# RWKV-7 attention followed by a hard-swish feed-forward: 64-row turns from unit 4 on, and one PSUM pair in place of two single banks

## The chip, the cores and the metric

The program runs on one core of one Trainium2 chip. A core has TensorE (PE in the profile: matmuls and transposes, and PEld, its weight loads), VectorE (DVE), ScalarE (ACT), GpSimd (POOL) and SyncE (SP, which only issues DMAs here). PE writes to PSUM, 8 banks of 512 float32 columns on 128 partitions; DVE and ACT read from there. The metric is the device time of one execution in microseconds (us).

## The reference

Everything is float32. Four batches, 8 heads, 768 tokens, head size 40. First a recurrence over tokens, per batch and head, with a 40x40 state:

```python
for t in range(S):
    y[:, :, t] = np.einsum('bhd,bhde->bhe', rt, state)
    Sa = np.einsum('bhde,bhe->bhd', state, at)
    state_decay = state * wt[:, :, None, :] - np.einsum('bhd,bhe->bhde', Sa, bt)
    state = state_decay + np.einsum('bhd,bhe->bhde', vt, kt)
```

Its output, laid out as 3072 tokens by 320 features, goes through a feed-forward layer with 2048 hidden features:

```python
h = x @ w_in
relu6 = np.clip(h + 3.0, 0.0, 6.0)
g = h * relu6 / 6.0
return g @ w_out
```

## The kernel before, in words

**Units.** The recurrence is done in chunks of 64 tokens. A *unit* is one chunk of two batches: 128 rows (64 tokens of each batch on 64 partitions) with 8 heads of 40 features. There are 24 units, 0 to 23 (`NK`), in groups of four (`NU`). The triangular systems of a group (64 by 64 for each head and batch) are inverted together on DVE, in some 60 small products and sums (`invert`, `prod` and `x` in the profile); the 64-blocks are completed from 32-blocks by two small PE steps (`third_block`, here z and t, each copied out of PSUM by four ACT copies, `zs` and `tinv`).

**The stages of a unit.** `prepare` makes a unit's own factors ahead of time: W turns the decay w (features onto partitions), copies it to the scan's input and DVE scans it (`prods`, L571); `gam` makes the running products; A, B and K turn a, b and k, and DVE multiplies each by a running product (`at` L615, `bt` L623, `kt` L703); F, E, EV and `factor` are further products. `step` does the recurrence: RT and VT turn r and v (ACT copies them out), S turns the state, R is at times the state (DVE adds EV, L888), C the masked scores of v and r (DVE masks them, L546), U and UT apply the inverse, rS is r times the state, H masked scores again, and `ysn` (L1021) yields the output and the new state; DVE adds both (L1028, L1032). move/move2 send the output by DMA to `xt`, the input of the feed-forward.

**Two kinds of turn.** `turn_pairs` makes four PE transposes of 128 rows by 128 columns (L486) into one PSUM bank. `turn_halves` makes eight of 64 rows by 128 columns (L496), on the upper and lower half of PE's rows by turns, into two banks, a pair. Before, a, b, r and v are turned by halves (a and b from unit 8, r and v from unit 4); w, k and the state always as 128 rows.

**Feed-forward jobs.** A job is (unit, half of the hidden features). `expand` makes 48 products (L1124) into two h banks, among them 16 of 64 rows (`short`); ACT and DVE make `gt` from each bank (L1139, L1140). `contract` (L1165) multiplies gt by w_out, 8 products of 320 columns. The contraction of a job is issued after the expansion of the next one. Before, the two jobs of a unit add up in the same bank `o`, and ACT copies the sum out once (`ob`, L1183), then two DMAs store it.

**The order.** It is written out by hand: each engine runs its instructions in the order in which the program issues them, and waits for semaphores on the way. From unit 4 on, four *blocks* j = 0 to 3 pass per unit. In each block `together` is called twice (the unit's own stages and those ahead); it issues the PE work of all its stages in the order of PRODUCTS, then the reads by ACT and DVE in the order of RESULTS. Between these calls `feed` issues pieces of the feed-forward at a rate given per block, with steps of the inversion beside them. In block 0 stand RT, VT, W and the ysn of the unit before; in block 1 S, A, B, R and C; in block 2 U, UT, rS, F; in block 3 H.

**PSUM.** From unit 2 on: bank `one` (128-row turns), bank `o` (feed-forward sums), two pairs `pair` (everything of the recurrence, `ps_pair`), two banks `h`. A tile of PSUM is given out again when the reads of its former owner are done, and its first PE write waits for that.

## Time and profile before

| | us |
|---|---|
| median of three runs (lowest, highest) | 787.39 (785.52, 788.26) |
| the profiled execution | 785.4 |
| its span, first to last instruction | 783.7 |
| PE busy | 725.0 |
| DVE busy | 486.6 |
| ACT busy | 320.2 |
| POOL busy | 171.9 |

By stretch of the span, PE's busy time and granted clock:

| stretch, us | PE busy | DVE busy | clock |
|---|---|---|---|
| 0 to 120 | 75.5 | 102.2 | 0.79 |
| 120 to 200 | 76.2 | 64.3 | 0.98 |
| 200 to 300 | 95.6 | 64.9 | 1.00 |
| 300 to 645 | 342.9 | 225.3 | 1.00 |
| 645 to 784 | 134.8 | 30.0 | 1.00 |

Unit 4 begins at about 190 us. In the profile a group's row gives busy time, the mean duration of one instruction, and the idle time of its engine ahead of it. A matmul's end is modelled and overlaps the next one's start, so what a group of matmuls costs PE is read from start to start in the timeline, not from its duration.

### The profile page before, as it was taken

How to read it: one execution, taken by the hardware profiler on the slowest of the kernel's cores; microseconds unless marked ns; L12 is line 12 of the kernel's file. 1: busy time of each engine (PE TensorE's matmuls, PEld its weight loads, DVE VectorE, ACT ScalarE, POOL GpSimd, SP SyncE). 2: the span in 40 equal slices, each digit the busy share in tenths (PEclk: the TensorE clock that was granted, in tenths of full speed). 3: DMA queues.
4: the chain of work that ended last, by engine and by line, in shares of the span. 5: the costliest groups of instructions: out<-in, count | busy, mean ns of one | idle time of the engine just before them, and what ended most of it. 6: DMA issues, size and time to landing. Idle time of an engine off the chain costs nothing.

```text
span 783.7 us, 32780 instructions
## 1 busy us (share of the span) xinstructions
PE 725.0 (93%) x14552; PEld 613.3 (78%) x14552; DVE 486.6 (62%) x951; ACT 320.2 (41%) x664; POOL 171.9 (22%) x321
## 2 busy tenths in 40 slices
PE   5636788999999989999999999999999999999998
PEld 3625677878878778888788888888888888888886
DVE  7899967688546699345888336887436972223110
ACT  2386865324445334443334543334543234412211
POOL 6403111222232304121304212203212111110000
PEclk9855899999999999999999999999999999999999
DMA  9684554311333312223213223213221101110000
GB/s 123 116 202 123 113 168 69 68 27 35 58 59 63 67 33 48 50 49 66 41 38 58 46 51 64 44 30 60 49 55 39 26 5 30 30 29 10 12 20 18
DMA packets 174205, 44.87 MB, mean 57 GB/s; under 512 B 157424, under 2 KB 172784, under 8 KB 174064
## 3 DMA queue, kind: packets, MB, share of 16 engines
q1 hardware_dynamic: 169760, 42.03, 27.5%
q8 instruction: 115, 1.88, 1.0%
q10 hardware_dynamic: 4304, 0.74, 0.6%
q14 instruction: 26, 0.21, 0.1%
HBM read 34.08 MB, written 3.93 MB: 49 GB/s over the span
## 4 chain that ended last, share of the span: by engine, by line
PE 77%; DVE 10%; issue 6%; DMA 2%; ACT 2%; POOL 2%; SPq 1%; POOLq 0%; ACTq 0%; DVEq 0%
PE h L1124 27%; PE o L1165 25%; PE pair L1021 4%; PE pair L524 4%; PE pair L496 2%; PE one L486 2%; DVE prods L571 2%; PE pair L884 2%; PE pair L925 1%; PE pair L717 1%; DVE prod L769 1%; PE pair L964 1%; DVE x L775 1%; PE pair L980 1%; PE one L906 1%
## 5 line engine op out<-in xcount | busy, mean ns | idle before, releaser
L1124 PE MATMUL h<-xt,win 128*128 128x128 f32 (+1 forms) x2304 | 248.7, 281 | 4.5 <-DVE gt L1140 4.5
L1124 PEld LDWEIGHTS h<-xt,win 128*128 128x128 f32 (+1 forms) x2304 | 229.3, 191 | 22.6 <-issue 4.2
L1165 PE MATMUL o<-wout,gt 128*128 128x320 f32 x768 | 230.5, 443 | 0.0
L1165 PEld LDWEIGHTS o<-wout,gt 128*128 128x128 f32 x768 | 138.4, 190 | 50.9 <-issue 0.2
L1140 DVE SCALAR_TENSOR_TENSOR gt<-gt,h 128x512 f32<-128x512 f32 x96 | 62.0, 680 | 73.4 <-ACT gt L1139 73.4
L1139 ACT ACTIVATE gt<-h,three 128x512 f32<-128x512 f32 x96 | 62.9, 687 | 102.8 <-PE h L1124 102.3
L546 DVE COPY_PREDICATED area<-mask,pair 128x512 f32<-128x512 int32 x56 | 40.4, 724 | 62.2 <-PE pair L524 52.8
L769 DVE TENSOR_TENSOR prod<-x 128x30 f32<-128x30 f32 (+9 forms) x180 | 65.5, 364 | 8.9 <-POOL x L754 3.3
L775 DVE TENSOR_TENSOR x<-x,prod 128x30 f32<-128x30 f32 (+9 forms) x180 | 64.3, 357 | 5.5
L1029 POOL TENSOR_TENSOR yg<-ys,gam 128x512 f32<-128x512 f32 x20 | 25.4, 1272 | 126.1 <-DVE ys L1028 83.2
L690 POOL TENSOR_TENSOR KBt<-K,rgt 128x320 f32<-128x320 f32 x22 | 19.1, 870 | 151.4 <-ACT rgt L679 139.9
L571 DVE TENSOR_TENSOR_SCAN prods<-area,start 128x528 f32<-128x528 f32 x24 | 40.8, 1703 | 9.7 <-ACT area L567 9.6
L1028 DVE TENSOR_TENSOR ys<-pair,ys 128x512 f32<-128x512 f32 x20 | 13.8, 690 | 49.8 <-PE pair L1021 40.8
L862 ACT ACTIVATE RT<-pair 128x512 f32<-128x512 f32 x22 | 13.1, 597 | 54.5 <-PE pair L496 54.4
L722 ACT ACTIVATE EV<-pair 64x320 f32<-64x320 f32 x44 | 18.9, 430 | 36.9 <-PE pair L717 36.5
L1021 PE MATMUL pair<-area,KBt 64*64 64x104 f32 x1280 | 33.1, 252 | 0.0
L1183 ACT ACTIVATE ob<-o 128x320 f32<-128x320 f32 x22 | 9.6, 437 | 56.2 <-PE o L1165 37.8
L837 ACT ACTIVATE tinv<-pair 32x256 f32<-32x256 f32 x48 | 18.0, 375 | 34.7 <-PE pair L827 34.2
L582 DVE TENSOR_TENSOR_SCAN area<-area,start 128x528 f32<-128x528 f32 x24 | 31.1, 1297 | 0.8
L1021 PEld LDWEIGHTS pair<-area,KBt 64*64 64x64 f32 x1280 | 29.1, 133 | 1.4
L950 POOL COPY area<-V 128x320 f32<-128x320 f32 x20 | 9.1, 455 | 84.6 <-DVE area L612 52.9
L600 POOL COPY rgam<-prods 128x256 f32<-128x256 f32 x22 | 24.9, 1131 | 0.0
(286 smaller groups left out, 1049.9 us busy)
## 6 DMA issues: line engine op xcount, KB each, us to landing
V<-in_v_dram SPq DMA_DIRECT2D x96, 40.0 KB
out_dram<-ob SPq DMA_DIRECT2D x47, 80.0 KB
R<-in_r_dram SPq DMA_DIRECT2D x92, 40.0 KB
B<-in_b_dram SPq DMA_DIRECT2D x42, 80.0 KB
K<-in_k_dram SPq DMA_DIRECT2D x42, 80.0 KB
W<-in_w_dram SPq DMA_DIRECT2D x37, 80.0 KB
A<-in_a_dram SPq DMA_DIRECT2D x37, 80.0 KB
xt<-yg SPq DMA_DIRECT2D x72, 40.0 KB
```

The lines of the kernel that those rows point to most:

```text
L524: nc.tensor.matmul(out=o[i][half(q), n ^ (2 * q * placed), :], lhsT=lhs[half(i, D), n ^ (2 * q * swap), half(q)], rhs=rhs[half(i, D), n, h ...
L546: nc.vector.copy_predicated(out=x[:].rearrange("p (i h) t -> p i h t", i=2), mask=mask8, data=o[2])
L571: nc.vector.tensor_tensor_scan(out=prods[:].rearrange("p r m i -> p (r m i)"), data0=wm[:, 0:SCAN], data1=start[:], initial=0.0, op0=ALU.m ...
L582: nc.vector.tensor_tensor_scan(out=back, data0=back, data1=start[:], initial=0.0, op0=ALU.mult, op1=ALU.add)
L769: nc.vector.tensor_tensor(out=pv, in0=_ap(x[:], (i + 1) * L + i, [[L, n], [0, i]]), in1=_ap(x[:], i * L, [[0, n], [1, i]]), op=ALU.mult,)
L775: nc.vector.tensor_tensor(out=rest, in0=rest, in1=pv, op=ALU.add)
L1021: nc.tensor.matmul(out=both[q][half(s), pr, :], lhsT=o[name][half(q), h * D:h * D + SLOT], rhs=beside[name][half(q), 4 * rs + 2 * (s ^ (q ...
L1029: nc.gpsimd.tensor_tensor(out=yg[:], in0=m["ys"][:].rearrange("p r q t -> p r (q t)"), in1=o["G"][:], op=ALU.mult)
L1124: nc.tensor.matmul(out=hp[c][:, i, :], lhsT=lhsT, rhs=rhs, start=(begun[c] == 0), stop=(begun[c] == 3 * NQ - 1))
L1139: nc.scalar.activation(out=gt[:], in_=hp[c][:], func=AF.Relu, bias=three[:], scale=1.0)
L1140: nc.vector.scalar_tensor_tensor(out=gt[:], in0=gt[:], scalar=6.0, in1=hp[c][:], op0=ALU.min, op1=ALU.mult)
L1165: nc.tensor.matmul(out=op[:], lhsT=gts[c][:, n, :], rhs=wout[:, c * HJ + r * NQ + n, :], start=((split or r == 0) and c == 0 and n == 0), ...
```

## The change

It concerns units 4 to 23. The state (unit 4 on), w and k (unit 8 on) are turned as 64-row halves into a pair. `factor` turns 40 in place of 64 rows of each half. The banks `one` and `o` are given back before unit 4, and a third pair, `third`, takes their place. It is the first pair that a `together` call of a unit's own stages takes in blocks 0 and 1 (so W and RT, or S and A, lie in it), and `contract` takes it for its sum. Since no sum can stay there, each job's sum leaves PSUM: the first job's is copied by ACT to an SBUF tile `part`, the second is added to it by DVE, which makes `ob`. `settle` issues the rest of a begun contraction before blocks 0 and 1; the pieces so issued are taken off the following `feed`. In block 1 the turn of k moves up behind that of b. The deferred 64-row products (`short`) come ahead of the turns, no longer behind them.

```diff
+    single = tc.tile_pool(name="single", bufs=1, space=PSUM, side="right")
+    alone = single.__enter__()
     def bank(tag, shape, bufs):
-        return ps.tile(shape, F32, name=tag, tag=tag, bufs=bufs)
+        return alone.tile(shape, F32, name=tag, tag=tag, bufs=bufs)
...
+    def begun_third():
+        single.__exit__(None, None, None)
+        pools["third"] = ctx.enter_context(tc.tile_pool(name="third", bufs=1, space=PSUM, side="right"))
...
         def w_stage():
-            wt = turn_pairs(o["WN"])
+            wt = turn_halves(o["WN"])[2] if halves else turn_pairs(o["WN"])
...
+            if halves:
+                for n in range(2):
+                    x = wt[:, :, :, n * HB:(n + 1) * HB]
+                    nc.scalar.activation(
+                        out=wv[:, :, n, 1:HB + 1].rearrange("p (r q) i -> p q r i", q=2),
+                        in_=x if n else x[:, :, :, ::-1], func=AF.Copy)
+                scan(wm)
+                return
...
         def factor_stage():
             if halves:
-                rg = ps_pair(NPR, SLOT)
+                rg = ps_pair(NPR, D)
...
         def k_stage():
-            x = turn_pairs(o["KN"])
+            x = turn_in(o["KN"], halves)
             yield PE
             kt = o["kt"] = turned("kt")
-            nc.vector.tensor_tensor(out=kt[:], in0=x[:], in1=o["rg"][:], op=ALU.mult)
+            for y, z, g in zip(parts_of(kt, halves), x, parts_of(o["rg"], halves)):
+                nc.vector.tensor_tensor(out=y, in0=z[:], in1=g, op=ALU.mult)
...
         def s_S():
+            if i >= NU:
+                sp = ps_pair(NPR, D)
+                for n in range(NPR):
+                    for x in range(2):
+                        nc.tensor.transpose(
+                            out=sp[x][:, n, :], identity=ident[half(x, D), half(x, D)],
+                            in_=st[half(x, D), n // 2, 2 * (n % 2):2 * (n % 2) + 2, :].rearrange("p r d -> p (r d)"))
+                yield PE
+                S = m["S"] = beside["S"]
+                nc.scalar.activation(out=S[:].rearrange("p q j (x d) -> p x (q j) d", x=2)[:, :, :, 0:D], in_=sp[2],
+                                     func=AF.Copy)
+                return
...
     def contract(i, r, gts):
-        split = i < SPLIT
-        if r == 0 or split:
+        spill = "third" in pools
+        split = i < SPLIT or spill
+        if spill:
+            op = pools["third"].tile([P, 2, 512], F32, name="third", tag="third", bufs=1)[:, 0, 0:DM]
+        elif r == 0 or split:
             op = bank("o", [P, 512], 1)[:, 0:DM]
         else:
             op = sums.pop(i)
+        held[0] = "contract"
...
             if split:
-                part = ffn.tile([P, 3 * P], F32, name="part", tag="xt", bufs=6)[:, 0:DM]
+                part = beside["part"] if spill else \
+                    ffn.tile([P, 3 * P], F32, name="part", tag="xt", bufs=6)[:, 0:DM]
                 nc.scalar.activation(out=part, in_=op[:], func=AF.Copy, scale=1.0 / 6.0)
...
+    def settle():
+        while held[0]:
+            owed[0] -= 1
+            next(stream)
...
-    AHEAD_STAGES = [["W", "gam"], ["A", "B"], ["F", "K"], ["E", "factor"], [], [], [],
+    AHEAD_STAGES = [["W", "gam"], ["A", "B", "K"], ["F"], ["E", "factor"], [], [], [],
                     ["EV"]]
...
-    PRODUCTS = ["W", "S", "K", "RT", "VT", "A", "B", "factor",
-                "ysn", "EV", "R", "C", "U", "UT", "rS", "H", "E", "F"]
-    RESULTS = ["RT", "ysn", "W", "VT", "EV", "R", "S", "C", "A", "B", "move", "move2",
-               "U", "UT", "rS", "F", "K", "H", "E", "factor", "gam"]
+    PRODUCTS = ["W", "RT", "VT", "S", "A", "B", "K", "factor",
+                "EV", "ysn", "R", "C", "U", "UT", "rS", "H", "E", "F"]
+    RESULTS = ["RT", "ysn", "W", "VT", "EV", "R", "S", "A", "B", "C", "K", "move", "move2",
+               "U", "UT", "rS", "F", "H", "E", "factor", "gam"]
...
-    def together(stages):
+    def together(stages, wide):
         begun, banks = [], 0
+        pairs.clear()
+        pairs.extend([("third", 1)] * wide + [("pair", 2)] * 2)
+        if narrow and spread[0] and stages:
+            narrow[0]()
...
-            together(part)
+            together(part, k == 0 and m % BLOCKS < 2)
...
     m = 0
+    settle()
     begun_beside()
+    begun_third()
...
+            if j < 2:
+                settle()
             parts = a_block(m)
```

## The prediction

> **What bounds the kernel now.** I read the page first: the slices and the chain of waits.

> ```profile
> PE 725.0 (93%) x14552; PEld 613.3 (78%) x14552; DVE 486.6 (62%) x951; ACT 320.2 (41%) x664; POOL 171.9 (22%) x321
> ...
> PE   5636788999999989999999999999999999999998
> ...
> PEclk9855899999999999999999999999999999999999
> ...
> PE 77%; DVE 10%; issue 6%; DMA 2%; ACT 2%; POOL 2%; SPq 1%; POOLq 0%; ACTq 0%; DVEq 0%
> ```

> From 200 us on PE is nearly always busy at full clock. So PE time removed there is time gained, and a wait put into PE's queue is time lost, since everything behind it waits too. Next, the groups kept apart by shape, for the reads of PSUM:

> ```profile
> L1183 ACT ACTIVATE ob<-o 128x320 f32<-128x320 f32 x22 | 9.6, 437 | 56.2 <-PE o L1165 37.8 <-issue 18.2
> ```

> Last, the timelines of PE and of DVE around one unit late in the run (columns: start, length, what, how many):

> ```profile
> 472.03 2.05 PE L1124 MATMUL h<-xt,win 128*128 128x128 f32 x16
> 473.92 1.24 PE L1165 MATMUL o<-wout,gt 128*128 128x320 f32 x4
> 475.00 0.60 PE L906 MATMUL one<-ident,state 128*128 128x128 f32 x4
> 475.53 0.46 PE L496 MATMUL pair<-ident,A 64*128 64x64 f32 x8
> 475.82 0.41 PE L496 MATMUL pair<-ident,B 64*128 64x64 f32 x8
> ...
> 477.26 3.50 PE L1165 MATMUL o<-wout,gt 128*128 128x320 f32 x12
> 480.60 0.60 PE L486 MATMUL one<-ident,K 128*128 128x128 f32 x4
> 481.12 0.68 PE L925 MATMUL pair<-RR,tinv 64*64 64x40 f32 x32
> ```

> ```profile
> 472.24 0.69 DVE L1028 TENSOR_TENSOR ys<-pair,ys 128x512 f32<-128x512 f32 x1 [3.92 <-ACT VT L895]
> 473.24 2.15 DVE L571 TENSOR_TENSOR_SCAN prods<-area,start 128x528 f32<-128x528 f32 x1
> 475.71 1.32 DVE L582 TENSOR_TENSOR_SCAN area<-area,start 128x528 f32<-128x528 f32 x1
> 477.52 1.27 DVE L1140 SCALAR_TENSOR_TENSOR gt<-gt,h 128x512 f32<-128x512 f32 x2
> 478.72 0.48 DVE L888 TENSOR_TENSOR RR<-pair,EV 128x320 f32<-128x320 f32 x1
> 479.12 0.71 DVE L546 COPY_PREDICATED area<-mask,pair 128x512 f32<-128x512 int32 x1
> 479.75 0.67 DVE L615 TENSOR_TENSOR at<-pair,gam 128x512 f32<-128x512 f32 x1
> 480.34 0.68 DVE L623 TENSOR_TENSOR bt<-pair,rgam 128x512 f32<-128x512 f32 x1
> ```

> Two things are to be seen. PE runs without a gap because between a product and its reader stand feed-forward products that wait for nothing (here 12 of `contract` between C and U). And DVE works through a queue of some 8 us behind `ysn` (472.24 to some 480.4, when `bt` is half done), so what is put behind this queue is late.

> **Gain: the turns.** A turn as 128 rows takes .53 us from start to start (S 475.00 to 475.53, K 480.60 to 481.12); one by halves takes .29 (A to B) or .35 (B to R). The difference is about .25. W of units 8 to 23 is 16 turns, K the same, S of units 4 to 23 is 20: 52 x .25 = 13.0, and .3 for the narrower `factor`: **-13.3**. The number of feed-forward products stays. Bounds: .18 x 52 = 9.4, and 14.

> **Cost: waits on PE.** The feed-forward sums no longer stay in PSUM. `settle` puts all that is left of a contraction ahead of blocks 0 and 1, and the turn behind it goes into the bank that the contraction has just filled. Before, unit 10 ran "contract x2, S, A, B, R, C, contract x6, K, U"; after, it runs "contract x8, S, A, B, K, R, C, U". The products that covered the reads stand in front of them. I walked the changed order unit by unit with the durations of before, and sort the waits by their cause.

> *A, the sum read directly before the turn that needs its bank* (14 places behind `settle`, and the last contraction): the last of 8 products starts, .5 later its end can be read, less the .29 that one takes anyway: .2. ACT's copy .44, or DVE's addition .48 (as the row of L888, same shape). The return to PE .1. That makes .75 a place, 15 x .75 = 11.3. In units 10, 14 and 18 one `gt` more stands on DVE ahead of it, +.25 each: **+12.0**. Bounds: 15 x .5 = 7.5 (the copy alone), 15 x 1.1 = 16.

> One row of the trace bears on this: a turn by halves takes .29 us and the read that empties its bank .44 to .72. [...]

> *B, DVE is late for the addition.* With E the end of `ysn`, its queue is ys .6, state .4, scans 2.15 + .28 + 1.38, gam and rgam .5, so E + 5.5, with two gt E + 6.75; inversion steps take .43 each. `ob` waits behind whatever was issued before. Before S: unit 7 3.85 (scans and gt), units 11 and 15 2.45 each. Before W: unit 8 2.0, units 12 and 16 .5 each. **+11.8**; low 7 (if the inversion steps run earlier), high 15.

> *C, contraction waits for a turn in `third`.* Unit 4 1.15 (ACT's two copies of W), units 8 and 12 2.3 each (`at` on DVE, behind scan and mask): **+5.75**; low 3.5, high 8.

> *D, a pair is held by DVE's reads.* Behind C, PE now goes to U, t or K at once, and the pair that it needs is free only after R's addition .4, at .65, bt .6 and the mask .7. Units 9 and 13 2.3 - .42 (what stood there before) each, 17 1.4, 10 and 14 2.7 each, 18 .8, 16 2.7, 4 1.45: 3.8 + 1.4 + 5.4 + .8 + 2.7 + 1.45 = **+15.5**. Low 8 (half, if the queue has been worked off during an earlier wait), high 20.

> *E, ACT is late.* The four copies `tinv` take 1.2 and must precede U: units 8 and 12 .35, 16 and 20 1.5 each (3.7); unit 5 waits for the six F copies and a mask, 2.2 + .8 + .4 + .65 (4.05): **+7.75**; low 3, high 9.

> *F, waits of before that go:* DVE's at units 7 and 16, 1.07 + 1.62 - .85 + .23: **-2.1**.

> Sum of the waits: 12.0 + 11.8 + 5.75 + 15.5 + 7.75 - 2.1 = +50.7; low 7.5 + 7 + 3.5 + 8 + 3 - 2 = 27, high 16 + 15 + 8 + 20 + 9 - 1 = 67. All durations are of one execution, 785.4 (span 783.7, and 1.7 around it): 785.4 - 13.3 + 50.7 = 822.8. The median of the runs is 2.0 above that execution, so I say **824** (between 823 and 825). The ends: 785.4 - 14 + 27 = 798, 785.4 - 9.4 + 67 = 843.

> **What costs nothing on the path.** The first job's `part` takes ACT the .44 that `ob` took; ACT is at 41%. DVE gets 20 additions x .49 = 10 us, at 62% busy with long idle times outside the queue of B; were there none, all 10 would be added. POOL gets one memset. The stores of `ob` are as many as before on SP's queue, at the end of the second job as before; with the hardware queue's packets at 27.5% of its engines' time, a store later by a microsecond has the next unit to land. K's turn moves past R and C, its `kt` behind the mask; its data came units before. The `short` products moved ahead of the turns change places with them alone.

> **The rivals.**

> *1. The clock falls as well (about 837).* The windows of before, with the columns stretch, length, busy time of PE, PEld, DVE, ACT and POOL, clock, DMA share and GB/s:

> ```profile
> 121.00:124.50 3.50, 2.06 (x45) 1.57 (x38) 3.43 (x7) 3.37 (x6) 0.00 (x0) 1.00 0.36 65
> 159.50:163.00 3.50, 1.97 (x67) 1.38 (x66) 3.29 (x7) 0.10 (x1) 3.47 (x7) 1.00 0.04 7
> 163.00:166.50 3.50, 3.50 (x39) 2.23 (x39) 3.26 (x10) 1.20 (x4) 0.05 (x1) 0.51 0.53 94
> ```

> A stretch with PE busy 1.97 of 3.5 was followed by one at clock .51; 2.06 at 121 kept 1.00 within it. 13 of the waits above are 1.5 us or longer, and where two meet in one stretch, PE may fall under that level. One stretch at half clock costs 3.5 / 2 = 1.75 us; 8 of the 13 make 14: 823 + 14 = 837. Against it: PE is busy without a gap on either side of a wait, so 1.5 to 2.3 us alone leaves 1.2 to 2.0 of 3.5, at the level of the row, not clearly under. [...]

> *2. The waits merge (about 802).* What DVE and ACT work off while PE stands for one reason is not waited for again: B, C and D are the same DVE queue, 33 us in sum. If only a third of it stays and A and E are at 9 and 5, the waits are 11 + 9 + 5 + 3 for the first blocks - 2 = 26 to 30, so 798 to 802. For it: a wait of 2 us is five inversion steps of .43 that DVE gets done meanwhile. Against it: B is longest at units 7, 11 and 15, while D's longest lie at 10, 14 and 16; in one unit they hardly meet.

> *3. Not slower (about 777).* The first job's sum is read by ACT, which idles 59% of the time; the same could hold for DVE, if it runs ahead. The one mechanism: `ysn` comes earlier against `settle`, because each of PE's waits gives DVE the same time, so that its queue is worked off by the second `settle`. Then B, C and D fall to nothing and only A's return of .2 to .3 per place stays, some 5 us: 785.4 - 13.3 + 5 = 777. It decides as soon as all waits together are below 13.3, about a quarter of my sum. Against it: A alone is 12, from durations that no order changes.

> *4. Nothing to be measured.* Within .3% (2.4 us, about what a measurement of this kernel can tell from no change) the waits would have to come to 11 to 16.

> **How the numbers follow.** My sum .50, clock .28, merged waits .12, not slower .07, nothing .03. So slower by over .3% has .90, faster .07, within .3% .03. The time of the likeliest is 824. 8 times in 10 is held from 802 (which cuts the lower half of rival 2, and rivals 3 and 4, .16 together) to 843 (the high end of the sum, and the middle of rival 1; above it some .05).

> **What the profile after would show.** Gain: 128x128 turns of W, K and S only before unit 8 (S: 4), the rows of halves longer by 52 x 8, at .28 to .35 a turn. A: PE idle ahead of S and of W, released by ACT `part` or DVE `ob`, about .75 each. B: the wait before S at units 7, 11 and 15 over 2 us, released by `ob`. C: the first `contract` of units 8 and 12 idle, released by `at`. D: U, t or z idle about 2.5 us at units 9, 10, 13, 14 and 16, released by the mask. E: U at 16 and 20 behind `tinv`. PE's busy time down by about 13, its idle time after 200 us up by about 50. If the busy time rises instead at a clock below 1.00, rival 1 holds. The prediction fails most easily in D and B, where I carried DVE's queue through whole units: an order of arrival other than that of before moves each by its whole size.

## The result, and the profile after

The changed kernel takes 855.5 us (median of 4 runs, 849.0 to 858.0) against 786.6 for the kernel before: 1.086 times as long, 95% interval 1.079 to 1.093. The forecast was slower, 824 us, 802 to 843. The direction was right; the time lies 12 us above the range, and the loss is 69 us where 37 were forecast.

The page of the changed kernel: span, busy times, the slices of PE and of the granted clock, and the chain that ended last.

```profile
span 856.0 us, 33201 instructions
...
PE 749.9 (88%) x14760; PEld 635.5 (74%) x14760; DVE 496.3 (58%) x972; ACT 319.8 (37%) x664; POOL 172.0 (20%) x322
...
PE   5627879988989899998898898989899999999997
...
PEclk9857799997969999998989998999799999999999
...
PE 53%; DVE 12%; issue 5%; ACT 2%; POOL 1%; DVEq 0%; POOLq 0%; ACTq 0%
```

PE's busy time went up by 24.9 us (725.0 to 749.9), although each turn by halves is shorter. PE's idle time, span less busy time, went from 58.7 to 106.1, up by 47.4. And where the row of the clock held 9s from unit 4 on, it now has 7s, 8s and a 6.

The groups kept apart by shape: the reads of the sums, and three products that now wait (the last column is idle time of the engine just before them, and what ended it).

```profile
L1217 ACT ACTIVATE area<-third 128x320 f32<-128x320 f32 x21 | 9.2, 437 | 38.6 <-PE third L1205 29.4 <-issue 9.1
...
L1222 DVE SCALAR_TENSOR_TENSOR ob<-third,area 128x320 f32<-128x320 f32 x21 | 10.1, 482 | 34.7 <-PE third L1205 30.3 <-issue 4.4
...
L1205 PE MATMUL third<-wout,gt 128*128 128x320 f32 x688 | 205.6, 448 | 8.0 <-ACT area L574 3.8 <-DVE at L639 3.4 <-ACT area L1217 0.6
...
L961 PE MATMUL pair<-RR,tinv 64*64 64x40 f32 x640 | 16.6, 243 | 7.5 <-DVE area L558 5.5 <-ACT tinv L862 1.5 <-issue 0.5
...
L852 PE MATMUL pair<-zs,tt 32*32 32x32 f32 x768 | 11.4, 213 | 11.7 <-DVE area L558 6.4 <-ACT F L684 2.2 <-ACT zs L837 1.7
...
L932 PE MATMUL third<-ident,state 40*128 40x40 f32 x160 | 8.6, 232 | 14.0 <-DVE ob L1222 12.9 <-ACT area L1217 1.1
```

S (L932) waits 14.0 us in all, for `ob` nearly always; U (L961) and t (L852) wait for the mask (L558); the contraction (L1205) for W's copies in unit 4 and for `at`. Before, the contraction, S and U had none and t 2.8 us.

The timelines of one place: PE from the end of a contraction over the `ysn` of unit 12 (492.31) to t in unit 13, and then DVE behind that `ysn`.

```profile
488.79 2.05 PE L1205 MATMUL third<-wout,gt 128*128 128x320 f32 x7
491.42 0.46 PE L504 MATMUL third<-ident,W 64*128 64x64 f32 x8 [0.58 <-DVE ob L1222]
491.72 0.41 PE L504 MATMUL third<-ident,R 64*128 64x64 f32 x8
491.96 0.41 PE L504 MATMUL pair<-ident,V 64*128 64x64 f32 x8
492.31 1.66 PE L1057 MATMUL pair<-area,KBt 64*64 64x104 f32 x64
494.09 0.75 PE L829 MATMUL pair<-tb,F 32*32 32x32 f32 x64
494.77 2.25 PE L1160 MATMUL h<-xt,win 128*128 128x128 f32 x24
496.86 0.39 PE L932 MATMUL third<-ident,state 40*128 40x40 f32 x8
497.07 0.44 PE L504 MATMUL third<-ident,A 64*128 64x64 f32 x8
497.35 0.42 PE L504 MATMUL pair<-ident,B 64*128 64x64 f32 x8
497.60 0.42 PE L504 MATMUL pair<-ident,K 64*128 64x64 f32 x8
497.95 0.68 PE L909 MATMUL pair<-state,at 40*64 40x40 f32 x32
...
499.04 1.16 PE L1160 MATMUL h<-xt,win 128*128 128x128 f32 x8
501.78 0.74 PE L852 MATMUL pair<-zs,tt 32*32 32x32 f32 x64 [1.58 <-DVE area L558]
```

```profile
494.03 0.69 DVE L1064 TENSOR_TENSOR ys<-pair,ys 128x512 f32<-128x512 f32 x1 [2.27 <-PE pair L1057]
...
495.04 2.15 DVE L595 TENSOR_TENSOR_SCAN prods<-area,start 128x528 f32<-128x528 f32 x1
...
499.31 0.48 DVE L913 TENSOR_TENSOR RR<-pair,EV 128x320 f32<-128x320 f32 x1
499.74 0.66 DVE L639 TENSOR_TENSOR at<-third,gam 128x512 f32<-128x512 f32 x1
...
500.32 0.67 DVE L647 TENSOR_TENSOR bt<-pair,rgam 128x512 f32<-128x512 f32 x1
500.92 0.71 DVE L558 COPY_PREDICATED area<-mask,pair 128x512 f32<-128x512 int32 x1
```

Two of the waits of the prediction are to be seen here: W behind `ob` (A, 491.42), and t behind a DVE queue without a gap, from `ys` at 494.03 to the end of the mask at 501.63 (D). And the gain: W takes .30 from start to start where 128 rows took .53, S .21, K .35.

Last, windows of the changed kernel around the wait of U in unit 10 (stretch, length, busy time of PE, PEld, DVE, ACT and POOL, clock, DMA share, GB/s). The record of the clock changes only on a grid of 3.413 us, so the stretches are cut on it.

```profile
391.53:394.94 3.41, 0.86 (x60) 0.75 (x53) 2.90 (x6) 0.00 (x0) 0.46 (x1) 1.00 0.38 80
394.94:398.36 3.42, 2.77 (x99) 2.58 (x91) 0.00 (x0) 0.93 (x2) 0.00 (x0) 0.50 0.11 29
398.36:401.77 3.41, 3.41 (x18) 3.29 (x17) 0.80 (x1) 2.51 (x7) 0.00 (x0) 0.50 0.20 39
289.13:292.54 3.41, 2.16 (x24) 1.85 (x24) 3.14 (x11) 0.00 (x0) 0.00 (x0) 1.00 0.01 2
292.54:295.96 3.42, 1.29 (x42) 1.23 (x44) 3.25 (x10) 0.44 (x1) 0.00 (x0) 1.00 0.02 5
```

A wait (the first line) is followed by two windows at half clock: the second is still at .50, though PE is busy 2.77 us of the 3.42 of the first, with products of 40 and 64 rows. The last two lines are of another place: PE is busy less, 2.16 of 3.41, with 8 records of 128 rows by 128 columns and 16 of 64 by 128, and the clock is still 1.00 in the window behind. In sum the trace has 82 us at half clock between 190 us and the end of the span, where the kernel before has none.

The span grew by 72.3 us. Three terms are read from the trace behind 190 us. PE's idle time grew from 10.5 to 55.7, +45.2. PE's busy time grew from 583.1 to 610.3; 76.4 of the 610.3 lie in windows at half clock, and if these products took twice their time, the clock made +38.2 of it. What is left of the busy time, -11.0, is the gain of the shorter turns. The last two terms are estimates: they hang on that factor of two. By the changed kernel's trace the contraction takes .269 us from start to start at full clock and .533 at half, a record of h .112 and .213 (medians), a product of L532, C among them, .0148 and .0262 (means); so 38.2 is the high end. e12 has the same .269 and .533 for its added products.

### The profile page after: what moved, and what is told of

Its sections match the earlier page's. It is cut to its first block, busy times and chain, and to the rows that moved or that the text cites. A ratio compares the mean times of both kernels' runs of the same rounds, so it can differ in the third digit from the quotient of the medians.

```text
span 856.0 us, 33201 instructions
## 1 busy us (share of the span) xinstructions
PE 749.9 (88%) x14760; PEld 635.5 (74%) x14760; DVE 496.3 (58%) x972; ACT 319.8 (37%) x664; POOL 172.0 (20%) x322
## 4 chain that ended last, share of the span: by engine, by line
PE 53%; DVE 12%; issue 5%; ACT 2%; POOL 1%; DVEq 0%; POOLq 0%; ACTq 0%
PE h L1160 20%; PE third L1205 15%; PE pair L532 3%; PE pair L1057 2%; DVE prods L595 2%; PE pair L961 2%; DVE gt L1176 2%; PE third L504 1%; DVE x L800 1%; DVE prod L794 1%; PE pair L1000 1%; PE pair L504 1%; PE pair L1016 1%; DVE area L606 1%; DVE ob L1222 1%
## 5 line engine op out<-in xcount | busy, mean ns | idle before, releaser
L1160 PE MATMUL h<-xt,win 128*128 128x128 f32 (+1 forms) x2304 | 266.1, 293 | 4.9 <-DVE gt L1176 4.9
L1160 PEld LDWEIGHTS h<-xt,win 128*128 128x128 f32 (+1 forms) x2304 | 246.7, 201 | 22.3 <-DVE gt L1176 6.8
L1205 PE MATMUL third<-wout,gt 128*128 128x320 f32 x688 | 205.6, 448 | 8.0 <-ACT area L574 3.8
L1205 PEld LDWEIGHTS third<-wout,gt 128*128 128x128 f32 x688 | 128.1, 194 | 57.4 <-ACT area L574 3.9
L1176 DVE SCALAR_TENSOR_TENSOR gt<-gt,h 128x512 f32<-128x512 f32 x96 | 62.3, 680 | 73.8 <-ACT gt L1175 73.7
L558 DVE COPY_PREDICATED area<-mask,pair 128x512 f32<-128x512 int32 x56 | 40.6, 726 | 83.8 <-PE pair L532 72.8
L595 DVE TENSOR_TENSOR_SCAN prods<-area,start 128x528 f32<-128x528 f32 x24 | 40.8, 1704 | 13.1 <-ACT area L574 12.0
L937 ACT ACTIVATE S<-third 128x320 f32<-128x320 f32 x20 | 8.7, 437 | 84.6 <-PE third L504 50.1
L1064 DVE TENSOR_TENSOR ys<-pair,ys 128x512 f32<-128x512 f32 x19 | 13.1, 690 | 46.1 <-PE pair L1057 29.8
L606 DVE TENSOR_TENSOR_SCAN area<-area,start 128x528 f32<-128x528 f32 x24 | 31.3, 1305 | 0.8
L1222 DVE SCALAR_TENSOR_TENSOR ob<-third,area 128x320 f32<-128x320 f32 x21 | 10.1, 482 | 34.7 <-PE third L1205 30.3
L887 ACT ACTIVATE RT<-third 128x512 f32<-128x512 f32 x20 | 11.9, 597 | 48.8 <-PE third L504 48.8
```

Source lines behind the costliest of these rows:

```text
L558: nc.vector.copy_predicated(out=x[:].rearrange("p (i h) t -> p i h t", i=2), mask=mask8, data=o[2])
L595: nc.vector.tensor_tensor_scan(out=prods[:].rearrange("p r m i -> p (r m i)"), data0=wm[:, 0:SCAN], data1=start[:], initial=0.0, op0=ALU.m ...
L606: nc.vector.tensor_tensor_scan(out=back, data0=back, data1=start[:], initial=0.0, op0=ALU.mult, op1=ALU.add)
L1160: nc.tensor.matmul(out=hp[c][:, i, :], lhsT=lhsT, rhs=rhs, start=(begun[c] == 0), stop=(begun[c] == 3 * NQ - 1))
L1176: nc.vector.scalar_tensor_tensor(out=gt[:], in0=gt[:], scalar=6.0, in1=hp[c][:], op0=ALU.min, op1=ALU.mult)
L1205: nc.tensor.matmul(out=op[:], lhsT=gts[c][:, n, :], rhs=wout[:, c * HJ + r * NQ + n, :], start=((split or r == 0) and c == 0 and n == 0), ...
```

## The experiments

All beside the kernel before on the same chip. PE's idle time and the time at half clock are of the profiled execution, behind 190 us of its span, where the change acts. The half clock goes to the end of the clock's record, so its last 1 to 5 us lie behind the last product in every run.

| run | time, us | ratio, 95% interval | PE idle | half clock |
|---|---|---|---|---|
| before | 786.6 | | 10.5 | 1.4 |
| changed | 855.5 | 1.086 (1.079 to 1.093) | 55.7 | 84.2 |
| e1, cover | 865.2 | 1.098 (1.095 to 1.101) | 62.3 | 94.2 |
| e2, ACT reads both sums | 846.0 | 1.075 (1.070 to 1.080) | 49.3 | 87.4 |
| e3, sums per job alone | 789.6 | 1.002 (1.001 to 1.004) | 12.6 | 2.2 |
| e4, w and k by halves alone | 800.1 | 1.015 (1.012 to 1.018) | 21.4 | 11.8 |
| e5, C twelve times | 969.9 | one run | 53.9 | 128.3 |
| e6, wide twenty times | 954.4 | one run | 10.9 | 0.7 |
| e7, changed, no scans | 841.2 | 1.070 (1.064 to 1.075) | 47.5 | 59.6 |
| e8, before, no scans | 780.8 | one run | 7.2 | 1.2 |
| e9, at and bt read first | 852.6 | 1.082 (1.077 to 1.088) | 55.1 | 70.0 |
| e10, e2 and e9 | 838.5 | 1.067 (1.062 to 1.071) | 47.8 | 62.7 |
| e11, spare products, two places | 844.2 | 1.072 (1.069 to 1.075) | 47.9 | 60.8 |
| e12, narrow twenty times | 1097.6 | one run | 10.7 | 275.1 |
| e13, spare products, eight places | 832.0 | 1.057 (1.053 to 1.061) | 40.1 | 19.5 |
| e14, e10 and spare products | 828.4 | 1.052 (1.049 to 1.055) | 39.1 | 15.9 |

### Each part of the change alone: e3 and e4

e3, on the kernel before: both jobs' sums leave PSUM, from their own bank.

```diff
-        split = i < SPLIT
+        if r == 0 and "part" in beside:
+            parted.add(i)
+        spill = i in parted
+        split = i < SPLIT or spill
...
-                part = ffn.tile([P, 3 * P], F32, name="part", tag="xt", bufs=6)[:, 0:DM]
+                part = beside["part"] if spill else \
+                    ffn.tile([P, 3 * P], F32, name="part", tag="xt", bufs=6)[:, 0:DM]
```

> The kernel before, with one part of the change alone: each job's sum leaves PSUM, the first copied to `part` by ACT, the second added by DVE; the banks, the turns and the order stay, and no contraction is settled early. Theory 1 (the reads cost nothing while a contraction has its own bank, since the next one starts an expansion later): 785 to 790 us, within .5% of the kernel before. Rival (DVE's 20 more reads of .49 or their waits are the cost by themselves): 796 us or more.

Measured: 789.6, +2 us. DVE's 20 additions and the extra reads cost next to nothing as long as the sum has a bank of its own.

e4, on the kernel before: w and k by halves into the two pairs. The new bodies of `w_stage`, `k_stage` and `factor_stage` are those of the change; the order is:

```diff
-    PRODUCTS = ["W", "S", "K", "RT", "VT", "A", "B", "factor",
-                "ysn", "EV", "R", "C", "U", "UT", "rS", "H", "E", "F"]
+    PRODUCTS = ["S", "RT", "VT", "A", "B", "factor",
+                "ysn", "W", "EV", "R", "C", "U", "UT", "rS", "H", "E", "F", "K"]
-    TURNS = PRODUCTS[:3]
+    TURNS = PRODUCTS[:1]
```

> The kernel before, with the other part alone, as far as two pairs carry it: w and k turned by halves into the two pairs from unit 8 on (w behind ysn, k behind F), the state as 128 rows into its bank; sums stay in `o`, nothing is settled early. 32 turns x .25 = 8 us less PE time. Theory 1 (turns by halves are a gain where they wait for nothing, and they don't lower the clock): 777 to 783 us, clock after 200 us 1.00. Rival (small products lower the clock by themselves, or two pairs are too few and K or W waits): 786 us or more, clock below 1.00 after 200 us or PE idle time up by 8 us or more.

Measured: 800.1, slower by 12.5 and not faster by 8. Both halves of this are visible. In unit 4 the turn of k, put behind other work, waits 5.28 us, by the trace for the DMA of k; with shorter waits around it the ysn of unit 4 comes 11 us later than before. And from the ysn of unit 8 to that of unit 19, where nothing of the kind happens, the kernel before takes 319.8 us and this one 320.8: no gain from 32 shorter turns. The timeline of e4 shows why:

```profile
446.16 0.68 PE L661 MATMUL pair<-bt,at 40*64 40x64 f32 x31
446.95 0.46 PE L496 MATMUL pair<-ident,K 64*128 64x64 f32 x8
447.34 1.34 PE L1177 MATMUL o<-wout,gt 128*128 128x320 f32 x4
```

A lone turn by halves takes .39 from start to start (446.95 to 447.34), and the 40-row product ahead of it .79 where it takes .58 when a 128-row product follows. That makes .39 and .21 more, .60 against the .53 of 128 rows: nothing is gained. In the changed kernel the halves stand in a row (W, R, V; S, A, B, K), and there one takes .24 to .34 by the median. So the halves pay by being put side by side, which the third pair allows here. What causes the .1 to .2 us more at these two changes of shape is shown by no run.

### The waits: e1, e2, e7, e8, e9 and e10

e1 covers A: two expansion pieces between the settled contraction and the turn.

```diff
+        begun = held[0]
         while held[0]:
             owed[0] -= 1
             next(stream)
+        for _ in range(2 if begun and available() else 0):
+            owed[0] -= 1
+            next(stream)
```

> The changed kernel, with two expansion pieces (8 products of 128x128, .9 us) issued between the end of a contraction that `settle` has finished and the turn behind it. Theory 1 (the waits of A to E cost PE about 47 us, and where a wait falls into a stretch of small products the next 3.41 us run at half clock, 38 us in sum): A falls from .75 to nothing at nearly all of its 15 places (-11) and B shrinks by up to .9 at 6 places (-5); a few half-clock windows go with them (-4 to -9); pieces missing later add up to 3. 830 to 840 us. Rival (the pieces taken from behind the turns are missed there just as much, so that the waits only move): 850 to 856, idle time of PE unchanged at about 106.

Measured: 865.2, 10 us slower than the changed kernel. A went in the main: of 16 waits of .5 to .9 us in front of S, W or R, 6 are left, and none in unit 13. B stayed: S still waits 3.38, 2.10 and 2.11 us at units 7, 11 and 15. The pieces took 1.8 us and not the .9 expected, since each product makes two records in the profile (16 of .112). The wait of t in unit 13 grew from 1.58 to 4.15 us. The same unit in e1, PE and then DVE:

```profile
490.60 1.66 PE L1057 MATMUL pair<-area,KBt 64*64 64x104 f32 x64
492.38 0.75 PE L829 MATMUL pair<-tb,F 32*32 32x32 f32 x64
493.06 0.44 PE L932 MATMUL third<-ident,state 40*128 40x40 f32 x8
...
495.25 0.67 PE L532 MATMUL pair<-RT,VT 40*64 40x64 f32 x32
500.08 1.08 PE L852 MATMUL pair<-zs,tt 32*32 32x32 f32 x64 [4.15 <-DVE area L558]
```

```profile
493.32 2.17 DVE L595 TENSOR_TENSOR_SCAN prods<-area,start 128x528 f32<-128x528 f32 x1
...
499.22 0.71 DVE L558 COPY_PREDICATED area<-mask,pair 128x512 f32<-128x512 int32 x1
```

From the start of `ysn` to the start of t it is 9.47 us in the changed kernel (492.31 to 501.78) and 9.48 here (490.60 to 500.08): DVE's queue sets that distance, whatever PE does in it. Products put ahead of `ysn` are missing behind it. The rival holds as to the mechanism: the wait moved. The time is 9 us above its range; PE idles 7 us more than in the changed kernel, and more windows are at half clock (94 us).

e2 takes the addition off DVE.

```diff
-                nc.vector.scalar_tensor_tensor(out=ob[:], in0=op[:], scalar=1.0 / 6.0,
-                                               in1=sums.pop(i), op0=ALU.mult, op1=ALU.add)
+                nc.scalar.activation(out=ob[:], in_=op[:], func=AF.Copy, scale=1.0 / 6.0)
+                nc.gpsimd.tensor_tensor(out=ob[:], in0=ob[:], in1=sums.pop(i), op=ALU.add)
```

> The changed kernel, with the second job's sum also copied out of PSUM by ACT (into ob), and POOL adding the first job's part to it in SBUF; DVE's 20 additions go. Theory 1: B goes (-11.8: the waits of 2.1 to 3.4 before S at units 7, 11 and 15 shrink to .7), the 1.0 waits of A become .75, and the half-clock windows behind those B waits go (about 7 of 24, -10): 830 to 838 us. Rival (the bank is not what the turn waits for there; DVE is late for the next step anyway, so the wait moves to R, at or U): idle time of PE about as before, 848 to 856. Rival 2 (ACT or POOL late in DVE's place): waits before S released by ACT, longer than .75.

Measured: 846.0, a gain of 9.5 where 17 to 25 were expected. From ysn to ysn unit 11 fell from 41.4 to 36.2 and unit 15 from 39.8 to 35.1 (before: 35.7 both), so B is what the prediction said there. In unit 7 the wait of S went too, and R and EV took it over (1.28 us idle for DVE's mask, and 1.66 us that the profile puts to "issue"). The time at half clock did not fall (87.4): windows went at units 11 and 15 and came at others. The profiled execution is the slowest of the four (852.9); by the granted clocks of all four the mean time at half clock over the span is 128 us, as in the changed kernel. Theory 1 is right on the waits and wrong on the windows, which do not go one by one with them.

e7 shortens DVE's queue itself: from unit 8 on it leaves out the running products of the decay (the first scan is a copy, the second is nothing). e8 is the same on the kernel before.

```diff
+            if i >= 2 * NU:
+                nc.vector.tensor_copy(prods[:].rearrange("p r m i -> p (r m i)"), wm[:, 0:SCAN])
+                return
             nc.vector.tensor_tensor_scan(
...
-            nc.vector.tensor_tensor_scan(out=back, data0=back, data1=start[:], initial=0.0,
-                                         op0=ALU.mult, op1=ALU.add)
+            if i < 2 * NU:
+                nc.vector.tensor_tensor_scan(out=back, data0=back, data1=start[:], initial=0.0,
+                                             op0=ALU.mult, op1=ALU.add)
```

> The changed kernel, with DVE's scans of units 8 to 23 left out (the first replaced by a copy of the same shape, the second by nothing): the running products of the decay are not computed. DVE's queue behind ysn is some 3.1 us shorter. Theory 1 (the waits of B, C and D are this queue, laid open when the products that covered it were put ahead; they set the half-clock windows): the waits at units 7 to 16 behind `ob`, `at` and the mask lose 1.5 to 3 each, some 18 of PE's 56 us of idle time after 190 us, and half of the 84 us at half clock goes: 855 - 18 - 20 = 810 to 825 us. Rival (the waits are the return through PSUM and ACT's reads, or other work of DVE): 845 to 855 us.

> The kernel before with the same scans left out, as the comparison. Both theories: its queue on DVE is covered by feed-forward products, so 50 us less work on DVE gives 780 to 787 us.

Measured: 841.2 and 780.8. The copy still takes 1.1 us where the first scan took 1.9, and the second scan took 1.3. So the queue is 2.1 us shorter a unit and not 3.1, and DVE's busy time fell by 29 us (496.3 to 467.2, and 486.6 to 457.1), not by 50 as both expectations reckon. This gives the changed kernel 14 us and the kernel before 6. The time lies between the two theories, nearer to the rival, but with a queue shortened by less than they assume it decides little. The waits of S at units 11 and 15 fell from 2.1 to 1.1 us, that of S at unit 7 from 3.4 to 2.2; U's wait at unit 10 stayed at 2.55 to the hundredth, so the scans had nothing to do with that one.

e9 goes for that wait.

```diff
-    RESULTS = ["RT", "ysn", "W", "VT", "EV", "R", "S", "A", "B", "C", "K", "move", "move2",
+    RESULTS = ["RT", "ysn", "W", "VT", "EV", "S", "A", "B", "R", "C", "K", "move", "move2",
```

> The changed kernel, with one line of the order of the reads altered: DVE reads the turned a and b (at, bt) ahead of R's addition, no longer behind it. In units 10, 14 and 16 the trace of the changed kernel has DVE idle for 2.4 us in front of R's addition, with a and b turned long before, and then PE idle for 2.55 while DVE does addition, at, bt and mask. Theory 1 (what is left of D is this order of reads): those waits fall from 2.55 to about 1.3, that is 3 to 5 places x 1.3, and some of the 8 half-clock windows behind them go: 838 to 850 us. Rival (DVE is late for at and bt as well, because gam or the turns are late): the waits stay at 2.5, 852 to 857 us.

Measured: 852.6, which can't be told from the changed kernel. U's wait fell from 2.55 to 2.15 only. DVE's timeline of e9 has the reason:

```profile
392.26 0.69 DVE L639 TENSOR_TENSOR at<-third,gam 128x512 f32<-128x512 f32 x1 [2.00 <-PE pair L909]
392.87 0.68 DVE L647 TENSOR_TENSOR bt<-pair,rgam 128x512 f32<-128x512 f32 x1
393.47 0.48 DVE L913 TENSOR_TENSOR RR<-pair,EV 128x320 f32<-128x320 f32 x1
393.87 0.71 DVE L558 COPY_PREDICATED area<-mask,pair 128x512 f32<-128x512 int32 x1
```

Placed first, `at` still waits for PE's product R (L909). My reading of DVE's idle time as a matter of order was wrong: by the code, `at` is prepared five units ahead in five buffers, so its tile is the one that R is just reading. That is argued from the code; no run with a sixth buffer was made. What stays is four reads in a row behind R, .4 + .6 + .6 + .7, the price that the prediction gave D.

e10 puts e2 and e9 together (both diffs).

> Both orders of reads together: the sums read by ACT (as in the run where ACT reads both) and at, bt ahead of R's addition. If the two causes are separate, their gains add: 10 us for the one, what the run with at and bt first shows for the other, 825 to 838 us, PE's idle time after 190 us at 40 to 45. If they are the same queue, no better than the better of the two.

Measured: 838.5, 17 us off, at the slow end of what was expected. 9.5 and 2.9 add to 12.4; the 4.6 us above that are within the spread of these kernels' runs (6 to 10 us). In the profiled execution PE's idle time fell by 8 us (55.7 to 47.8), and PE's busy time at half clock by 25 (76.4 to 51.8), which by the factor of two is worth 12, an estimate: of the gain more is clock than waits.

### The clock: e5, e6, e11, e12, e13 and e14

e5 and e6 ask what the clock goes by, on the kernel before.

```diff
-            x = scores(m["VT"], m["RT"])
+            x = scores(m["VT"], m["RT"], again=12 if i >= 2 * NU else 1)
...
-        for n in range(NPR):
+        for n in list(range(NPR)) * again:
```

> The kernel before, where the 32 products of C are issued twelve times over in units 8 to 23 (the same values into the same places): 5.5 us more of small products (40x64 and 64 columns) per unit, with PE busy throughout. It asks what the clock counts. If PE's busy time counts (the reading in the prediction), the clock after 200 us stays 1.00 and the time is 786 + 16 x 5.5 = 874 us. If the clock counts how much of the array works (the small products fill 16% of it), a stretch of 3.41 us full of them is followed by one at half clock in each of these units, one or two at a time: 16 x 1 or 2 x 1.7 = 27 to 55 more, 901 to 929 us, 55 to 110 us at half clock.

```diff
+        if r == 0 and i >= 2 * NU:
+            for _ in range(20):
+                nc.tensor.matmul(out=op[:], lhsT=gts[0][:, 0, :], rhs=wout[:, 0, :], start=True, stop=True)
```

> The same for wide products, as the other side of the run before: the kernel before, where the first product of each unit's first contraction (128x128 weights, 320 columns) is issued twenty times more in units 8 to 23, overwriting itself: 16 x 20 x .28 = 89 us. Both readings of the clock: 870 to 880 us, clock after 200 us 1.00.

Measured: 969.9 with 128 us at half clock for the small products, 954.4 with none for the wide ones. The 89 us expected of the wide ones were half of what they cost, since a product of this kind makes two records of .27 in the profile (PE has 640 records more); that is an error of my sum, not of the theory. (The same holds for `expand`: the 48 of a job are records, two for each of 24 products.) e5 is not as clean as it was meant to be: the small products follow each other at 14.6 ns, but the burst of unit 10 has gaps of .94 and 1.91 us that the profile puts to "issue", and the windows ahead of a fall have PE busy for some 2.1 of 3.41, so PE was not busy throughout.

e12 is the clean form: e6 with one size altered.

```diff
-                nc.tensor.matmul(out=op[:], lhsT=gts[0][:, 0, :], rhs=wout[:, 0, :], start=True, stop=True)
+                nc.tensor.matmul(out=op[:], lhsT=gts[0][0:L, 0, :], rhs=wout[0:L, 0, :], start=True, stop=True)
```

> The run with twenty wide products more, with one size altered: the added products have 32 rows in place of 128 (a quarter of the array), as many of them, as long, and as dense. If the clock counts PE's busy time: as the wide ones, 950 to 960 us, clock after 200 us 1.00. If it counts the share of the array at work: a window full of them is at .25 of 3.41 = .85 us and falls under the limit that all windows so far suggest (1.16 us): the 11 us of added products per unit run at half clock for the most part, 16 x 7 to 11 us more, 1060 to 1130 us, some 250 us at half clock.

Measured: 1097.6, 143 us more than e6, with as many records of the same length. The windows (first e6, then e12):

```profile
300.00:800.00 500.00, 497.85 (x8435) 406.94 (x8432) 234.16 (x448) 159.01 (x350) 85.02 (x147) 1.00 0.18 34
```

```profile
423.40:426.82 3.42, 3.42 (x15) 2.33 (x14) 3.25 (x9) 0.00 (x0) 0.00 (x0) 1.00 0.21 35
426.83:430.24 3.41, 3.41 (x8) 2.20 (x7) 0.66 (x2) 0.00 (x0) 0.00 (x0) 0.50 0.13 22
...
300.00:900.00 600.00, 597.75 (x8456) 457.24 (x8454) 236.88 (x450) 159.04 (x349) 87.34 (x149) 0.84 0.15 29
```

PE is busy for all of 423.40 to 426.82, at full clock, with the added products of 32 rows alone, and the next window is at .50. At full clock a record takes .269 us from start to start in both runs, so only the rows differ. PE's busy time is not what the clock goes by here: the fall to .50 comes behind a window in which PE is busy 3.42 us of 3.42.

e11 tests it in the changed kernel, by adding work in units 10 and 14 where PE waits for DVE.

```diff
+            if j == 2 and i in (2 * NU + 2, 3 * NU + 2):
+                spare = pools["h"].tile([P, NQ, P], F32, name="h", tag="h", bufs=2)
+                for _ in range(9):
+                    nc.tensor.matmul(out=spare[:, 0, :], lhsT=win[:, 0, 0:P], rhs=win[:, 0, P:2 * P],
+                                     start=True, stop=True)
```

> The changed kernel with work added: in units 10 and 14 nine products of 128x128 whose result nobody reads (18 records, 2.0 us) go into a free h bank between C and U, where PE waits 2.55 us for DVE. Theory 1 (a window of 3.41 us with too little of the array at work is followed by one at half clock): the wait shrinks to .5, the five half-clock windows behind these two places (394.9 to 401.8 and 528.1 to 538.3 us) shrink to none to two, units 10 to 11 and 14 to 15 end 2 to 4 us sooner each, the whole 4 to 8 us faster than the changed kernel in spite of the added work. Rival (the half-clock windows hang on something else): no change or 2 to 4 us slower, the windows stay.

Measured: 844.2, 11 us faster for 4 us of added work. The place in unit 10, and the windows over it:

```profile
389.39 0.67 PE L532 MATMUL pair<-RT,VT 40*64 40x64 f32 x32
390.00 2.27 PE L1547 MATMUL h<-win 128*128 128x128 f32 x18
392.62 0.68 PE L961 MATMUL pair<-RR,tinv 64*64 64x40 f32 x32 [0.35 <-DVE area L558]
```

```profile
390.66:394.07 3.41, 3.06 (x112) 2.90 (x114) 2.39 (x5) 0.22 (x1) 0.46 (x1) 1.00 0.39 86
394.07:397.48 3.41, 3.41 (x70) 3.34 (x61) 0.33 (x1) 3.22 (x9) 0.00 (x0) 1.00 0.09 22
```

U starts as far behind C as before (3.2 us), but the windows at half clock behind it are gone: units 10 and 14 take 31.3 us from ysn to ysn, where the changed kernel took 35.1 and 35.0. The gain beyond these 7.4 us came at other units: the time at half clock fell by 23.4 us (84.2 to 60.8), of which the five windows behind these two places are 17.1.

e13 fills eight places.

```diff
+    def spare(name, n):
+        shape = [P, NQ, P] if name == "h" else [P, 2, 512]
+        x = _ap(pools[name].tile(shape, F32, name=name, tag=name, bufs=2)[:], 0, [[1, P]])
+        for _ in range(n):
+            nc.tensor.matmul(out=x, lhsT=win[:, 0, 0:P], rhs=win[:, 0, P:2 * P], start=True, stop=True)
...
+            if j == 1 and i in (7, 11, 15):
+                spare("pair", 13 if i == 7 else 8)
+            if j == 2 and i in (10, 14):
+                spare("h", 9)
...
+                if j == 1 and i in (4, 5, 16):
+                    spare("h", 5 if i == 4 else 9)
                 block(i, j)
```

> The changed kernel with spare 128x128 products (nobody reads them) at eight places where PE waits 1.5 to 3.5 us for a read and a half-clock window follows: before t in units 4, 5 and 16, before S in units 7, 11 and 15, before U in units 10 and 14. No wait of the kernel is shortened by it; only the array is at work meanwhile. If the miss of the prediction is the clock alone (the sum of the waits, 823 us, being right), most of the half-clock time after 190 us (84 us) goes and 5 to 8 windows stay at places that are not filled: 822 to 832 us. If the waits themselves are longer than the sum had them, the clock comes back to 1.00 but the time stays above 838.

e14 is e10 with the spare products of units 4, 5, 16, 10 and 14. Those before S are left out, since ACT's reading leaves S no long wait.

> Both orders of reads (sums read by ACT; at and bt ahead of R's addition) with spare products before t in units 4, 5 and 16 and before U in units 10 and 14. If waits and clock are two separate terms, the gains add: the two orders took 15 to 17 us off, of the 63 us at half clock some 40 go: 838 - 18 = 818 to 826 us. If the reads' gain was a gain of the clock in the first place, it is no better than the run with eight places. In neither case as fast as the kernel before (787): A's .7 at 14 places and the waits for DVE stay.

Measured: 832.0 and 828.4. The spare products of e13 are 140 records, 17.4 us of PE's time. With them counted as idle time PE idles 57.5 us behind 190 us, where the changed kernel idles 55.7: the waits in sum became no shorter, and yet the kernel is 23.5 us faster. In e13 17 us at half clock are left inside the span's work, worth at most 8.5 us by the factor of two: without any, 823 to 832. So by this estimate some 36 to 45 of the 69 us are waits, less the gain of the turns, and 24 to 32 the clock.

e14 is 3.6 us faster than e13 and 2.4 above the range of "the gains add", so by its time it decides between neither. The traces tell more: idle time and spare products come to 49.6 us, 8 less than in e13, as e10 has 8 less than the changed kernel. The orders of reads are worth 8 us of waits in either case; the rest of what they gained in e10 was clock, which the spare products gain as well.

No run of the changed kernel was faster than the kernel before.

## Why the prediction was right or wrong

**The gain** (-13.3) was right by the rows of the turns. From start to start, at full clock and where nothing waits behind it, a turn of W takes .28 us on the mean, of S .30, of K .33, and of B, no longer last of its row, .26 in place of .34. That is .25 x 16 + .23 x 20 + .20 x 16 + .08 x 16 = 13.1 us. What the rows don't show is what the products beside a turn lose (.21 us in e4). PE's busy time has it in: by the factor of two 11.0 us are left of the gain in the changed kernel, and 7.4 in e13, where little half clock blurs the sum.

**The waits**, from the trace of the changed kernel, from start to start beyond what the products ahead take:

| step | forecast | measured |
|---|---|---|
| A, the sum read before a turn, 15 places | 12.0 | 12.0 (.69 to .80 each, 1.02 at units 10, 14, 18) |
| B, DVE late for `ob` | 11.8 | 10.0 (before S, unit 7: 3.5, 11 and 15: 2.3; before W, three of .6, and the 2.0 at unit 8 didn't come) |
| C, contraction waits for a turn | 5.75 | 7.3 (unit 4: 3.8 where 1.15 was put, 8 and 12: 1.75) |
| D, pair held by DVE | 15.5 | 14.2 (9, 13: 1.7; 10, 14, 16: 2.6; 4: 1.5; 17: .8; 18: .5) |
| E, ACT late | 7.75 | 5.7 (unit 5: 3.3, 16 and 20: 1.2) |

Together 49.2 of 52.8. That the sum is so near is in part luck: unit 4's wait, three times the size that was put, hides half of what B, D and E were too long. It is a wait behind ACT, whose two copies of W come after 2.1 us of `tinv`, two gt and RT; they were not put in its queue. That the cause is DVE's reads with the cover gone is shown by e1 (9.47 and 9.48 us) and, where the bank is concerned, by e3 against the changed kernel. For ACT's reads (E, and unit 4) it is read from the timelines alone.

**The step that failed is the clock, which the main sum put at nothing.** The text had it as rival 1, at +14 and with a chance of .28, and the range took the high end of the waits or the middle of rival 1, never the waits and the clock together. The waits came as counted and the clock came on top of them, with 24 us by e13's spare products and up to 38 by PE's busy time at half clock and the factor of two. Three things were wrong in the working of it.

First, the measure. It compares PE's busy time with 1.97 of 3.5 and concludes that a wait of 1.5 to 2.3 us, with PE busy on either side, lies "at the level of the row, not clearly under". But what stands on either side of these waits is turns, R and C, products of 40 and 64 rows, and they count for less (e12 shows it for 32 rows; for 40 and 64 it rests on the estimate below). The row of 1.97 had it to show: 64 of its 67 records are products of 40 and 64 rows.

Second, one window of 1.75 was put down for each drop. Behind seven of the thirteen places two to four windows in a row are at half clock (two are shown above, with PE busy 2.77 and 3.41 at .50). In the first of the two there are small products alone, which by the estimate below do not bring the clock back.

Third, 8 places of 13 were counted, though the list of waits has 14 of 1.5 us or longer. The clock fell at 13 places, 24 windows, one of them (unit 12, 476.87) behind a gap that no step had listed.

**Rival 2**, merged waits: did not happen, the idle time behind 190 us grew by 45.2 where the sum had 50.7. **Rival 3** (reads come early because PE's waits give DVE time): wrong by e1, where DVE's queue keeps its length behind `ysn`. **What costs nothing**: held, by e3, +2 us for the additions and the reads.

In the signs that were named, "PE's busy time down by about 13 ... if it rises instead at a clock below 1.00, rival 1 holds" is what the page showed: +24.9, at .92.

## What to carry to other kernels

Before products are moved ahead of a chain, ask what they covered: the distance from a product to its last reader on the other engine can be fixed by that engine's queue (9.5 us here), and then every product taken out of it comes back as a wait. Price such a wait twice where small products stand beside it: once as idle time (55.7 us here), and once as the half clock of the windows behind it (84.2 us of them here, an estimated loss of 24 to 38 us); useless wide products in a wait that can't be avoided may then make the kernel faster (11 us in e11). And cost a turn by the neighbours that it will have, not by the fastest row of its kind (.39 us alone in e4, .24 to .34 in a row).
